# Reordering the start of a fused linear-attention and SwiGLU kernel: tile 1's K products, its scaled x, and tile 6's statistics

## The chip, the cores and the metric

The kernel runs on one core of a Trainium2 chip. The metric is the device time of one execution in microseconds (us), taken as the median of several runs. A profile of one further execution shows what each engine did: PE (the matrix engine; PEld is its weight load), ACT (ScalarE), DVE (VectorE), POOL (GpSimd) and SP (the queue that issues most of the DMAs).

## The reference

With x of 2048 rows by 512 columns in bf16, the output is x plus two branches of the same layer-normalised x:

```
def reference(A_x, A_wqkv, A_wo, B_x, B_w_gate, B_w_up, B_w_down):
    x = A_x                                   # (1, 2048, 512)
    xn = _layernorm(x, axis=-1)               # (x - mean) / sqrt(var + 1e-5)
    return x + _A_ref(xn, A_wqkv, A_wo) + _B_ref(xn, B_w_gate, B_w_up, B_w_down)

# A: linear attention, 32 heads of 16
    q, k, v = split(xn @ wqkv)
    phi = lambda t: where(t > 0, t + 1, exp(t)) + 1e-6
    pq, pk = phi(q), phi(k)
    kv = sum over s of pk (x) v;   z = sum over s of pk
    o = (pq @ kv) / (pq . z + 1e-6);   return o @ wo
# B: SwiGLU with F = 1792
    return (silu(xn @ w_gate) * (xn @ w_up)) @ w_down
```

## The kernel before, in words

The 2048 rows are 16 tiles of 128 rows. The program has three stretches. In the first, each tile gets its statistics, its normalised rows `xn`, their transposed form, the products for K and Q, and the feature map of K; and the sum over rows of xn (transposed) times pk is accumulated in four PSUM banks (`gtacc`, four matmuls a tile). In the second, the small matrices of the attention are made from that sum, while the SwiGLU products of the first 512 rows run. In the third, the SwiGLU products of the other 512-row blocks alternate with the output products of finished tiles.

All order is written out by hand. Every helper appends operations to one list per engine, and a small recorder (`_Prog`) adds the semaphore waits that the named tiles require. So the order of the calls in the program is, for each engine, the order in its queue, and an engine that waits holds everything behind it. Moving a call changes something only against the calls of the same engine. Two DMA issues hang on moved calls: `xn(t)` is `xn_dve(t)` followed, for tiles from 3 on, by a DMA transpose issued by SP.

The first tiles have a way of their own, and the change lies there. Tiles 0 to 3 don't wait for the inverse standard deviation before their products: `xc` is x minus the mean, it is transposed (tiles 0 to 2 by PE, with copies by ACT or DVE, called `tp_block`/`tc_block` and `tp_first`/`tc_first`; tile 3 by a DMA, `transpose_xc`), and K and Q are multiplied from it by `proj_part` (one product of 128 x 512, L499) or `proj_first` (two, L486). A K or Q of a tile is four such products over the four slices of the 512 columns, summed in one bank. The scale `rstd` then goes into ACT's evaluation of the bank: `first_ek` (exponential, L556), `first_pk` (Relu, L562), `first_pq` (L574). `clip_k` (L539, DVE) limits the exponential, and `first_feat` (L588, DVE; for tile 0 `feat_pool`, L581, on POOL) adds the two into pk. The normalised rows for `gtacc` are made by `xn_dve` (L316, DVE), which needs `rstd`. Tiles from 4 on are projected from the DMA-transposed `xn` (L472).

The statistics of a tile are `bns` (L299) and `agg` (L302) on DVE, then on POOL `eps` (L327) and `rstd_of` (L336), or `eps_two` (L344) and `rstd_two` (L353) for two tiles in one instruction each. The running sum of pk is `zsum` on POOL (L612 for tile 0, L616 for the rest). PE begins with eight matmuls on constants (`fill`, L271) until its first operands are there.

In the first stretch PE's order is: transposes of tiles 0 and 1, the 12 products of L499 (K of tiles 0 and 1, the first two Q products of each), transposes of tile 2, the four left of L499, K and Q of tile 2, `gtacc(0)`, K and Q of tile 3, `gtacc(1)`, `gtacc(2)`, and then K and Q of tile t followed by `gtacc(t-1)` for t = 4 and on.

Of the kernel before, what the change touches and what calls it, by code (L numbers as in the profile page):

```python
# [109 lines left out]
def bass_parallel_sum__linear_attn_block__swiglu_ffn__prompt_kernel(  # L110
# [13 lines left out]
    pe, act, dve, pool, sp = nc.tensor, nc.scalar, nc.vector, nc.gpsimd, nc.sync  # L124
    bf, f32 = dt.bfloat16, dt.float32

    with contextlib.ExitStack() as es:
# [64 lines left out]
        def bk(i):  # L192
            return ("bank", i)
# [10 lines left out]
        def xload(eng, h, t0, n, after=()):  # L204
            K.dma(
                eng, lambda: h.dma_start(x_sb[:, t0:t0 + n, :], rows(xin, t0, n)),
                r=list(after), w=[("x", t0 + i) for i in range(n)],
            )
# [89 lines left out]
        def bns(t):  # L298
            K.op("dve", lambda: dve.bn_stats(stats[:, t, :], x_sb[:, t, :]), r=[("x", t)], w=[("st", t)])  # L299

        def agg(t):
            K.op("dve", lambda: dve.bn_aggr(mv[:, t, :], stats[:, t, :]), r=[("st", t)], w=[("mv", t)])  # L302
# [10 lines left out]
        def xn_dve(t):  # L313
            K.op(
                "dve",
                lambda: dve.tensor_scalar(  # L316
                    out=xn_sb[:, t, :], in0=x_sb[:, t, :], scalar1=mv[:, t, 0:1], scalar2=rstd[:, t:t + 1],
                    op0=ALU.subtract, op1=ALU.mult,
                ),
                r=[("x", t), ("mv", t), ("rstd", t)], w=[("xn", t)],  # L320
            )

        def eps(t, eng):
            h = dve if eng == "dve" else pool
            K.op(
                eng,
                lambda: h.tensor_scalar(  # L327
                    out=vpe[:, t:t + 1], in0=mv[:, t, 1:2], scalar1=1e-5, scalar2=None, op0=ALU.add,
                ),
                r=[("mv", t)], w=[("vpe", t)],  # L330
            )

        def rstd_of(t):
            K.op(
                "pool",
                lambda: pool.tensor_tensor(out=rstd[:, t:t + 1], in0=vpe[:, t:t + 1], in1=nhalf[:, 0:1], op=ALU.pow),  # L336
                r=[("vpe", t), ("nhalf",)], w=[("rstd", t)],
            )

        def eps_two(t, eng):  # L340
            h = dve if eng == "dve" else pool
            K.op(
                eng,
                lambda: h.tensor_scalar(  # L344
                    out=vpe[:, t:t + 2], in0=mv[:, t:t + 2, 1], scalar1=1e-5, scalar2=None, op0=ALU.add,
                ),
                r=[("mv", t), ("mv", t + 1)], w=[("vpe", t), ("vpe", t + 1)],
            )

        def rstd_two(t):  # L350
            K.op(
                "pool",
                lambda: pool.tensor_tensor(  # L353
                    out=rstd[:, t:t + 2], in0=vpe[:, t:t + 2], in1=nhalf[:, :], op=ALU.pow,
                ),
                r=[("vpe", t), ("vpe", t + 1), ("nhalf",)], w=[("rstd", t), ("rstd", t + 1)],
            )
# [65 lines left out]
        def xc_full(t):  # L423
            K.op(
                "dve",
                lambda: dve.tensor_scalar(
                    out=xc_sb[:, t, :], in0=x_sb[:, t, :], scalar1=mv[:, t, 0:1], scalar2=None, op0=ALU.subtract,
                ),
                r=[("x", t), ("mv", t)], w=[("xc", t, 0), ("xc", t, 1)],
            )  # L430
# [8 lines left out]
        def tp_first(t, h, b):  # L439
            tb = banks[b].bitcast(bf)[:, 0:HD].rearrange("p (c s) -> p c s", c=2)  # L440
            K.op(
                "pe",
                [
                    (lambda c=c: pe.transpose(  # L444
                        tb[:, c, :], xc_sb[:, t, (2 * h + c) * P:(2 * h + c + 1) * P], ident[:, :],
                    ))
                    for c in range(2)
                ],
                r=[("xc", t, h), ("ident",)], w=[bk(b)],
            )  # L450

        def tc_first(t, h, b):
            tb = banks[b].bitcast(bf)[:, 0:HD].rearrange("p (c s) -> p c s", c=2)
            K.op(
                "act",
                lambda: act.activation(xcT[:, NDC * t + 2 * h:NDC * t + 2 * h + 2, :], tb, ACT.Copy),
                r=[bk(b)], w=[("xcT", t, 2 * h), ("xcT", t, 2 * h + 1)],
            )

        def transpose_dma(t):  # L460
            K.dma(
                "sp",
                lambda: sp.dma_start_transpose(out=xnT[:, :, t * P:(t + 1) * P], in_=xn_sb[:, t, :]),
                r=[("xn", t)], w=[("xnT", t)],
            )
# [15 lines left out]
        def proj_first(t, wname, h):  # L481
            lo, b = (D, kb(t)) if wname == "wk" else (0, qb(t))
            K.op(
                "pe",
                [
                    (lambda c=c: pe.matmul(  # L486
                        banks[b], xcT[:, NDC * t + c, :], wqkv_sb[:, c, lo:lo + D],
                        start=(c == 0), stop=(c == NDC - 1),
                    ))
                    for c in (2 * h, 2 * h + 1)  # L490
                ],
                r=[("xcT", t, i) for i in (2 * h, 2 * h + 1)] + [(wname, i) for i in (2 * h, 2 * h + 1)], w=[bk(b)],
            )

        def proj_part(t, wname, c, pos):
            lo, b = (D, kb(t)) if wname == "wk" else (0, qb(t))
            K.op(
                "pe",
                lambda: pe.matmul(  # L499
                    banks[b], xcT[:, NDC * t + c, :], wqkv_sb[:, c, lo:lo + D],  # L500
                    start=(pos == 0), stop=(pos == NDC - 1),
                ),
                r=[("xcT", t, c), (wname, c)], w=[bk(b)],
            )

        def kb(t):
            return 2 * (t % 2)

        def qb(t):
            return 2 * (t % 2) + 1  # L510
# [43 lines left out]
        def first_ek(t):  # L554
            K.op(
                "act", lambda: act.activation(ek[:, t % NE, :], banks[kb(t)], ACT.Exp, scale=rstd[:, t:t + 1]),  # L556
                r=[bk(kb(t)), ("rstd", t)], w=[("ek", t % NE)],
            )

        def first_pk(t):  # L560
            K.op(
                "act", lambda: act.activation(kpos[:, t % NE, :], banks[kb(t)], ACT.Relu, scale=rstd[:, t:t + 1]),  # L562
                r=[bk(kb(t)), ("rstd", t)], w=[("kpos", t % NE)],
            )
# [27 lines left out]
        def clip_k(t):  # L592
            clip(ek[:, t % NE, :], ("ek", t % NE))
# [14 lines left out]
        def zsum(t, after=()):  # L608
            pk = pkq[:, t, 0, :]
            after = list(after)  # L610
            if t == 0:
                K.op("pool", lambda: pool.tensor_copy(zacc[:, :], pk), r=[("pk", t)] + after, w=[("zacc",)])  # L612
            else:
                K.op(
                    "pool",
                    lambda: pool.tensor_tensor(out=zacc[:, :], in0=zacc[:, :], in1=pk, op=ALU.add),  # L616
                    r=[("pk", t), ("zacc",)] + after, w=[("zacc",)],
                )
# [20 lines left out]
        def xn(t):  # L639
            xn_dve(t)  # L640
            if t >= 3:
                transpose_dma(t)
# [12 lines left out]
        tc_block(0, 0, 4, "dve")  # L655
        tc_block(0, 1, 5, "act")
        tp_first(0, 1, 6)
        tc_first(0, 1, 6)
        eps(0, "pool")
        tp_first(1, 0, 7)  # L660
        tp_first(1, 1, 3)
        tc_first(1, 0, 7)
        bns(1)
        rstd_of(0)
        xn_dve(0)
# [7 lines left out]
        agg(3)  # L673
        proj_part(0, "wk", 0, 0)
        proj_part(0, "wk", 1, 1)
        proj_part(0, "wk", 3, 2)
        proj_part(0, "wk", 2, 3)
        first_ek(0)
        clip_k(0)
        xc_full(3)  # L680
        bns(4)
        proj_part(1, "wk", 0, 0)
        proj_part(1, "wk", 1, 1)
        proj_part(1, "wk", 3, 2)
        proj_part(1, "wk", 2, 3)
        proj_part(1, "wq", 0, 0)
        proj_part(1, "wq", 1, 1)
        transpose_xc(3)
# [9 lines left out]
        agg(4)  # L698
        bns(5)
        agg(5)  # L700
        bns(6)
        agg(6)
        proj_part(0, "wq", 2, 2)
        proj_part(1, "wq", 2, 2)
        proj_part(0, "wq", 3, 3)
# [1 line left out]
        proj_part(1, "wq", 3, 3)  # L707
        proj_first(2, "wk", 0)
        proj_first(2, "wk", 1)
        eps_two(1, "pool")  # L710
        rstd_two(1)
        first_ek(1)
        clip_k(1)
        first_pq(1)
# [3 lines left out]
        gtacc(0)  # L718
        eps_two(3, "pool")
        rstd_two(3)  # L720
        eps_two(5, "pool")
        rstd_two(5)
        xn(4)
        xload("sp", sp, 12, 2)
        xn_dve(1)
        first_pk(1)
        first_feat(1)
        proj_first(3, "wk", 0)
# [5 lines left out]
        first_pk(2)  # L734
        first_feat(2)
        xn(5)
        xn(6)
        first_pq(2)
        proj_first(3, "wk", 1)
        first_ek(3)  # L740
# [3 lines left out]
        gtacc(1)  # L744
        gtacc(2)
        xn_dve(3)
        zsum(0, [("xn", 3)])
        bns(7)
        kproj(4)
# [374 lines left out]
```

## Time and profile before

| what | value |
|---|---|
| median of 3 runs | 210.42 us (210.4 to 210.62) |
| profiled execution, its own time | 210.88 us |
| span of the profiled execution, first to last instruction | 209.6 us |
| PE busy | 206.9 us, 99% of the span |
| DVE busy | 120.3 us, 57% |
| ACT and POOL busy | 71.3 and 72.0 us, 34% each |
| chain that ended last | PE 97%, DMA 1%, DVE 1% |

A row of the timeline gives start, length, engine, source line, operation, output and inputs, and the count of instructions merged into the row; in brackets the idle time of the engine before it and what ended that. A matmul's length in the record covers its way through the array, so successive matmuls overlap in it; what they cost the engine is the distance between starts. In the waits, a row is engine, line, whom it waited for, total time, times, and the longest.

### The profile page before, as it was taken

The page shows a single profiled execution, that of the slowest core. Times are in us where ns is not written, and L with a number is a line of the kernel's source. Part 1 is how long each engine was busy: PE and PEld are TensorE (multiplying, and loading weights), DVE is VectorE, ACT ScalarE, POOL GpSimd, SP SyncE. Part 2 cuts the span into 40 slices and gives each one's busy share as a digit, 9 for nine tenths or more (in the row PEclk, how much of TensorE's full clock was granted, in tenths as well). Part 3 has the DMA queues.
Part 4 walks back from the last instruction along what each step waited for, and adds up shares of the span by engine and source line. Part 5 has one row for each costly group of instructions (what it writes and reads, how often), then busy time and mean ns, then how long its engine had stood idle before and what let it go on. Part 6 is the DMA issues. An engine that isn't in the chain of part 4 may idle for free.

```text
span 209.6 us, 2822 instructions
## 1 busy us (share of the span) xinstructions
PE 206.9 (99%) x1014; PEld 94.5 (45%) x1014; DVE 120.3 (57%) x246; ACT 71.3 (34%) x126; POOL 72.0 (34%) x90
## 2 busy tenths in 40 slices
PE   8999999999999999999999999999999999999996
PEld 3444444444444444444444444444444444444444
DVE  4989989335465874637355746365556535374122
ACT  6686666976543331302122312213031213121000
POOL 3526977658032443223141422240424132221200
DMA  6763644697797021010101110102011010110101
GB/s 201 225 179 71 127 78 100 175 377 240 192 359 68 2 46 26 29 25 25 50 2 50 28 25 25 50 0 53 2 48 25 27 28 25 46 32 25 50 28 50
DMA packets 30287, 16.84 MB, mean 80 GB/s; under 512 B 20928, under 2 KB 29632, under 8 KB 30272
## 3 DMA queue, kind: packets, MB, share of 16 engines
q1 hardware_dynamic: 29984, 16.39, 29.9%
q10 hardware_dynamic: 288, 0.26, 0.4%
q8 instruction: 8, 0.13, 0.3%
q14 instruction: 7, 0.06, 0.1%
HBM read 9.70 MB, written 2.10 MB: 56 GB/s over the span
## 4 chain that ended last, share of the span: by engine, by line
PE 97%; DMA 1%; DVE 1%; issue 0%
PE psum L821 46%; PE psum L1026 23%; PE psum L472 10%; PE psum L1015 7%; PE psum L624 7%; PE psum L499 2%; PE psum L486 2%; DMA x_sb<-in_A_x_dram 1%; PE psum L444 0%; DVE stats L299 0%; PE psum L928 0%; PE psum L410 0%; PE psum L951 0%; DVE xc_sb L380 0%; DVE out_sb L1039 0%
## 5 line engine op out<-in xcount | busy, mean ns | idle before, releaser
L836 ACT ACTIVATE sg<-psum 128x512 bf16<-128x512 f32 x56 | 33.4, 598 | 106.0 <-PE psum L821 103.6
L821 PE MATMUL psum<-xnT,wg_sb 128*128 128x512 bf16 x224 | 57.5, 379 | 0.0
L821 PE MATMUL psum<-xnT,wu_sb 128*128 128x512 bf16 x224 | 57.5, 379 | 0.0
L970 POOL TENSOR_TENSOR prod<-pkq,zb 128x512 f32<-128x512 bf16 x16 | 18.6, 1161 | 55.9 <-DVE pkq L548 55.9
L821 PEld LDWEIGHTS psum<-xnT,wu_sb 128*128 128x128 bf16 x224 | 21.9, 98 | 26.4
L821 PEld LDWEIGHTS psum<-xnT,wg_sb 128*128 128x128 bf16 x224 | 21.7, 98 | 26.2 <-issue 0.2
L1039 DVE TENSOR_TENSOR out_sb<-psum,x_sb 128x512 bf16<-128x512 f32 (+2 forms) x17 | 11.2, 660 | 35.9 <-PE psum L1026 35.9
L994 POOL TENSOR_TENSOR pqn<-pkq,rden 128x512 bf16<-128x512 bf16 x16 | 16.9, 1055 | 36.6 <-DVE rden L988 36.6
L842 DVE TENSOR_TENSOR pkq<-psum,sg 128x512 bf16<-128x512 f32 x28 | 19.2, 686 | 17.1 <-PE psum L821 14.7
L842 DVE TENSOR_TENSOR xn_sb<-psum,sg 128x512 bf16<-128x512 f32 x28 | 18.8, 671 | 14.2 <-PE psum L821 13.6
L1026 PE MATMUL psum<-wd_sb,xn_sb 128*128 128x512 bf16 (+2 forms) x126 | 25.7, 355 | 0.0
L1026 PE MATMUL psum<-wd_sb,pkq 128*128 128x512 bf16 x112 | 25.5, 379 | 0.0
L472 PE MATMUL psum<-wqkv_sb,xnT 128*128 128x512 bf16 x96 | 22.5, 379 | 0.0
L616 POOL TENSOR_TENSOR zacc<-zacc,pkq 128x512 f32<-128x512 f32 x15 | 17.3, 1155 | 5.0 <-DVE ek L539 4.6
L1026 PEld LDWEIGHTS psum<-wd_sb,xn_sb 128*128 128x128 bf16 x126 | 11.8, 98 | 12.5
L1026 PEld LDWEIGHTS psum<-wd_sb,pkq 128*128 128x128 bf16 x112 | 11.0, 98 | 13.2
L1015 PE MATMUL psum<-m_sb,eq 128*128 128x512 bf16 (+2 forms) x68 | 16.6, 366 | 0.0
L624 PE MATMUL psum<-pkq,xn_sb 128*128 128x512 bf16 x64 | 15.9, 379 | 0.0
L472 PEld LDWEIGHTS psum<-wqkv_sb,xnT 128*128 128x128 bf16 x96 | 9.4, 98 | 11.3
L978 DVE TENSOR_REDUCE den<-prod 128x32 f32<-128x512 f32 x16 | 10.9, 683 | 5.9 <-POOL prod L970 5.9
L299 DVE BATCH_NORM_STATS2 stats<-x_sb 128x6 f32<-128x512 bf16 x16 | 10.9, 679 | 3.3 <-DMA x_sb<-in_A_x_dram 3.3
L548 DVE SCALAR_TENSOR_TENSOR pkq<-pkq,eq 128x512 bf16<-128x512 bf16 x16 | 11.1, 693 | 0.6
(73 smaller groups left out, 139.3 us busy)
## 6 DMA issues: line engine op xcount, KB each, us to landing
out_dram<-out_sb SPq DMA_DIRECT2D x15, 128.0 KB, 1.7
wg_sb<-in_B_w_gate_dram SPq DMA_DIRECT2D x2, 896.0 KB, 8.2
wu_sb<-in_B_w_up_dram SPq DMA_DIRECT2D x2, 896.0 KB, 6.4
wd_sb<-in_B_w_down_dram SPq DMA_DIRECT2D x1, 1792.0 KB, 11.1
x_sb<-in_A_x_dram SPq DMA_DIRECT2D x5, 256.0 KB, 3.0
x_sb<-in_A_x_dram SPq DMA_DIRECT2D x5, 128.0 KB, 3.2
wqkv_sb<-in_A_wqkv_dram SPq DMA_DIRECT2D x5, 128.0 KB, 3.4
wqkv_sb<-in_A_wqkv_dram SPq DMA_DIRECT2D x1, 512.0 KB, 8.4
```

Of the source, the lines that this page charges most:

```text
L472: (lambda c=c: pe.matmul(banks[b], xnT[:, c, t * P:(t + 1) * P], wqkv_sb[:, c, lo:lo + D], start=(c == 0), stop=(c == NDC - 1),))
L548: lambda: dve.scalar_tensor_tensor(out=dst, in0=src, scalar=0.0, in1=e, op0=ALU.max, op1=ALU.add,),
L616: lambda: pool.tensor_tensor(out=zacc[:, :], in0=zacc[:, :], in1=pk, op=ALU.add),
L624: (lambda c=c: pe.matmul(banks[4 + c], xn_sb[:, t, c * P:(c + 1) * P], pkq[:, t, 0, :], start=(t == 0), stop=(t == NT - 1),))
L821: (lambda c=c: pe.matmul(banks[b], w_sb[:, c, fc * P:(fc + 1) * P], xnT[:, c, C * 512:(C + 1) * 512], start=(c == 0), stop=(c == NDC - 1),))
L836: lambda: act.activation(sg[:, j % NSG, :], banks[gb], ACT.Silu),
L842: lambda: dve.tensor_tensor(out=hT(C, fc), in0=banks[ub], in1=sg[:, j % NSG, :], op=ALU.mult,),
L970: lambda: pool.tensor_tensor(out=p, in0=pkq[:, t, 1, :], in1=zb[:, :], op=ALU.mult),
L994: lambda: pool.tensor_tensor(out=pqn[:, t % NPN, :].rearrange("p (i g h e) -> p g i h e", i=NB, g=NG, e=DH), in0=pkq[:, t, 1, :].rearrange ...
L1015: (lambda g=g: pe.matmul(dst, pqnT(t)[:, g, :], m_sb[:, g, lo:hi], start=(g == 0), stop=False,))
L1026: (lambda fc=fc: pe.matmul(dst, hT(C, fc)[:, jj * P:(jj + 1) * P], wd_sb[:, fc, lo:hi], start=False, stop=(fc == NFC - 1),))
L1039: lambda: dve.tensor_tensor(out=o, in0=src, in1=x_sb[:, t, lo:hi], op=ALU.add),
```

## The change

It moves calls and splits one pair of instructions; no operand, shape, buffer or transfer is changed.

- ACT: the copy of tile 0's second transposed half, `tc_first(0, 1, 6)`, goes behind the copy of tile 1's first half. PE's transposes keep their order.
- PE: tile 1's first two K products go ahead of tile 0's last two. Over the eight K products the order was 0,0,0,0,1,1,1,1 and becomes 0,0,1,1,0,0,1,1.
- DVE: tile 1's scaled x (`xn_dve(1)`) moves from behind tile 4's scaled x to behind tile 3's subtraction, ahead of tile 4's statistics. The calls for its `rstd` move up in the program.
- DVE: tile 6's statistics move from behind tile 5's to behind tile 5's scaled x, after tile 2's feature sum. Tile 6's scaled x, with its DMA transpose, moves from there to behind tile 3's scaled x.
- POOL: `rstd` of tiles 5 and 6, one pair of instructions for both, becomes a pair for each.

```
@@ (before the first products)
         tp_first(0, 1, 6)
-        tc_first(0, 1, 6)
         eps(0, "pool")
         tp_first(1, 0, 7)
         tp_first(1, 1, 3)
         tc_first(1, 0, 7)
+        tc_first(0, 1, 6)
@@ (K products)
         proj_part(0, "wk", 0, 0)
         proj_part(0, "wk", 1, 1)
+        proj_part(1, "wk", 0, 0)
+        proj_part(1, "wk", 1, 1)
         proj_part(0, "wk", 3, 2)
         proj_part(0, "wk", 2, 3)
+        proj_part(1, "wk", 3, 2)
+        proj_part(1, "wk", 2, 3)
         first_ek(0)
         clip_k(0)
         xc_full(3)
+        eps_two(1, "pool")
+        rstd_two(1)
+        xn_dve(1)
         bns(4)
-        proj_part(1, "wk", 0, 0)
-        proj_part(1, "wk", 1, 1)
-        proj_part(1, "wk", 3, 2)
-        proj_part(1, "wk", 2, 3)
@@ (statistics)
         bns(5)
         agg(5)
-        bns(6)
-        agg(6)
@@
-        eps_two(1, "pool")
-        rstd_two(1)
         first_ek(1)
@@
-        eps_two(5, "pool")
-        rstd_two(5)
+        eps(5, "pool")
+        rstd_of(5)
         xn(4)
         xload("sp", sp, 12, 2)
-        xn_dve(1)
         first_pk(1)
@@
         first_pk(2)
         first_feat(2)
         xn(5)
-        xn(6)
+        bns(6)
+        agg(6)
+        eps(6, "pool")
+        rstd_of(6)
@@
         gtacc(1)
         gtacc(2)
         xn_dve(3)
+        xn(6)
         zsum(0, [("xn", 3)])
```

More of the change, by code (lines that the diff above doesn't have):

```diff
@@ L657, in bass_parallel_sum__linear_attn_block__swiglu_ffn__prompt_kernel @@
         tp_first(0, 1, 6)
-        tc_first(0, 1, 6)
         eps(0, "pool")
@@ L662, in bass_parallel_sum__linear_attn_block__swiglu_ffn__prompt_kernel @@
         tc_first(1, 0, 7)
+        tc_first(0, 1, 6)
         bns(1)
@@ L675, in bass_parallel_sum__linear_attn_block__swiglu_ffn__prompt_kernel @@
         proj_part(0, "wk", 1, 1)
+        proj_part(1, "wk", 0, 0)
+        proj_part(1, "wk", 1, 1)
         proj_part(0, "wk", 3, 2)
         proj_part(0, "wk", 2, 3)
+        proj_part(1, "wk", 3, 2)
+        proj_part(1, "wk", 2, 3)
         first_ek(0)
@@ L680, in bass_parallel_sum__linear_attn_block__swiglu_ffn__prompt_kernel @@
         xc_full(3)
+        eps_two(1, "pool")
+        rstd_two(1)
+        xn_dve(1)
         bns(4)
[L682 to L685, printed above, removed]
         proj_part(1, "wq", 0, 0)
@@ L700, in bass_parallel_sum__linear_attn_block__swiglu_ffn__prompt_kernel @@
         agg(5)
-        bns(6)
-        agg(6)
         proj_part(0, "wq", 2, 2)
@@ L709, in bass_parallel_sum__linear_attn_block__swiglu_ffn__prompt_kernel @@
         proj_first(2, "wk", 1)
-        eps_two(1, "pool")
-        rstd_two(1)
         first_ek(1)
@@ L720, in bass_parallel_sum__linear_attn_block__swiglu_ffn__prompt_kernel @@
         rstd_two(3)
-        eps_two(5, "pool")
-        rstd_two(5)
+        eps(5, "pool")
+        rstd_of(5)
         xn(4)
         xload("sp", sp, 12, 2)
-        xn_dve(1)
         first_pk(1)
@@ L736, in bass_parallel_sum__linear_attn_block__swiglu_ffn__prompt_kernel @@
         xn(5)
-        xn(6)
+        bns(6)
+        agg(6)
+        eps(6, "pool")
+        rstd_of(6)
         first_pq(2)
@@ L746, in bass_parallel_sum__linear_attn_block__swiglu_ffn__prompt_kernel @@
         xn_dve(3)
+        xn(6)
         zsum(0, [("xn", 3)])
```

## The prediction

> **What bounds the kernel now.** I read the page first (busy time, chain), then the waits of the matmul engine, then PE's timeline for the first 21 us, and only then the engines whose queues the change edits. From the page:
>
> ```profile
> span 209.6 us, 2822 instructions
> PE 206.9 (99%) x1014; PEld 94.5 (45%) x1014; DVE 120.3 (57%) x246; ACT 71.3 (34%) x126; POOL 72.0 (34%) x90
> ...
> PE 97%; DMA 1%; DVE 1%; issue 0%
> ```
>
> PE is busy for 206.9 of 209.6 us and carries 97% of the chain. A busy PE could still hide holes, because a matmul's record is longer than its slot, so I look at starts. The only wait of PE in the whole span, and its timeline:
>
> ```profile
> PE psum L271 <- PEq L1109: 0.8, 1, 0.8
> 0.84 3.36 PE L271 MATMUL psum<-const-bfloat16-1.0 128*128 128x512 bf16 x8 [0.84 <-PEq L1109]
> 4.26 0.40 PE L410 MATMUL psum<-ident,xc_sb 128*128 128x128 bf16 x2
> 4.46 0.84 PE L444 MATMUL psum<-ident,xc_sb 128*128 128x128 bf16 x6
> 5.09 3.52 PE L499 MATMUL psum<-wqkv_sb,xcT 128*128 128x512 bf16 x12
> 8.45 0.39 PE L444 MATMUL psum<-ident,xc_sb 128*128 128x128 bf16 x4
> ...
> 12.12 1.89 PE L486 MATMUL psum<-wqkv_sb,xcT 128*128 128x512 bf16 x8
> ...
> 15.57 1.89 PE L472 MATMUL psum<-wqkv_sb,xnT 128*128 128x512 bf16 x8
> ...
> 19.89 1.03 PE L624 MATMUL psum<-pkq,xn_sb 128*128 128x512 bf16 x4
> ```
>
> Between 12.12 and 15.57 the timeline has sixteen products (eight of L486, eight of L624): 3.45 / 16 = 0.216 us each; from 15.57 to 19.89 twenty products (two projections of eight and one accumulation of four) take 4.32, again 0.216. The stream has no hole there. Only the beginning is slower: 12 products from 5.09 to 8.45 take 3.36. If the last eight go at 0.216 (1.73), the first four took 1.63, some 0.41 each. So PE doubles its rate at about 6.7 us and then works without a break to the end. An edit gains only if it shortens the time before 4.26 (it touches nothing there) or brings the rate up earlier; it loses if one of PE's operands becomes late.
>
> **Part 1: the product order.** The same 1014 matmuls are issued. Of the 12 products, positions 3 and 4 become tile 1's first two, 5 and 6 tile 0's last two. Starts, from the steps of 0.41 and 0.216: 5.09, 5.50, 5.91, 6.31, 6.72, 6.93, 7.15, 7.37. Who feeds them is ScalarE:
>
> ```profile
> 4.91 0.94 ACT L456 ACTIVATE xcT<-psum 128x256 bf16<-128x256 bf16 x3
> 6.92 0.69 ACT L556 ACTIVATE ek<-psum,rstd 128x512 bf16<-128x512 f32 x1 [1.08 <-PE psum L499]
> 7.50 0.68 ACT L562 ACTIVATE kpos<-psum,rstd 128x512 f32<-128x512 f32 x1
> 8.76 0.66 ACT L456 ACTIVATE xcT<-psum 128x256 bf16<-128x256 bf16 x2 [0.57 <-PE psum L444]
> ...
> 11.24 0.70 ACT L562 ACTIVATE kpos<-psum,rstd 128x512 f32<-128x512 f32 x1
> 11.99 0.23 PEld L486 LDWEIGHTS psum<-wqkv_sb,xcT 128*128 128x128 bf16 x2 [0.20 <-ACT kpos L562]
> 1.73 0.46 SPq L213 DMA_DIRECT2D wqkv_sb<-in_A_wqkv_dram  x1
> DMA to landing us min/median/max: 3.0/3.4/3.7
> ```
>
> The three copies are 0.28 apart and 0.38 long. Tile 1's first half now goes first, but its transposes are the third and fourth of the six at L444: six of them take 5.09 - 4.46 = 0.63, so the fourth starts at 5.09 - 3 x 0.105 = 4.77 and ends, like the sixth (4.98 to 4.46 + 0.84 = 5.30), 0.32 later, at 5.09. So that copy runs 5.12 to 5.50, tile 0's second half 5.40 to 5.78, tile 1's second half 5.68 to 6.06. Position 3 needs the first at 5.91, position 5 the second at 6.72, position 7 the third at 7.15. All have 0.4 us or more in hand: no hole. Weights: the slice issued at 1.73 lands by 1.73 + 3.7 = 5.43 even at the longest landing, and was needed at 6.31, now at 6.93. Nothing waited for it, so this slack buys nothing.
>
> What comes later is tile 0's finished K: its sixth product instead of the fourth, 6.93 + 0.38 = 7.31 instead of 6.88. The exponential (L556) moves from 6.92 to 7.35, the Relu (L562) from 7.50 to 7.94, ending 8.62. ScalarE's next work at 8.76 waits 0.57 us for PE, so it covers the 0.43, and ScalarE is unchanged from there on.
>
> **Part 2: VectorE.** Its queue is in order, so I walk it:
>
> ```profile
> 7.87 0.26 DVE L539 TENSOR_SCALAR ek<-ek 128x512 bf16<-128x512 bf16 x1
> 8.04 0.35 DVE L426 TENSOR_SCALAR xc_sb<-x_sb,mv 128x512 bf16<-128x512 bf16 x1
> 8.69 0.69 DVE L299 BATCH_NORM_STATS2 stats<-x_sb 128x6 f32<-128x512 bf16 x1 [0.30 <-DMA x_sb<-in_A_x_dram]
> ...
> 10.31 0.66 DVE L299 BATCH_NORM_STATS2 stats<-x_sb 128x6 f32<-128x512 bf16 x1
> ...
> 11.10 0.26 DVE L539 TENSOR_SCALAR ek<-ek 128x512 bf16<-128x512 bf16 x1
> 11.28 0.73 DVE L316 TENSOR_SCALAR xn_sb<-x_sb,mv,rstd 128x512 bf16<-128x512 bf16 x2
> 11.97 0.69 DVE L588 TENSOR_TENSOR pkq<-kpos,ek 128x512 bf16<-128x512 f32 x1
> ...
> 13.73 0.73 DVE L316 TENSOR_SCALAR xn_sb<-x_sb,mv,rstd 128x512 bf16<-128x512 bf16 x2
> 14.82 0.29 DVE L539 TENSOR_SCALAR ek<-ek 128x512 bf16<-128x512 bf16 x1 [0.35 <-ACT ek L556]
> 15.40 0.69 DVE L588 TENSOR_TENSOR pkq<-kpos,ek 128x512 bf16<-128x512 f32 x1 [0.29 <-ACT kpos L562]
> 16.01 0.41 DVE L316 TENSOR_SCALAR xn_sb<-x_sb,mv,rstd 128x512 bf16<-128x512 bf16 x1
> 16.33 0.69 DVE L299 BATCH_NORM_STATS2 stats<-x_sb 128x6 f32<-128x512 bf16 x1
> ...
> 18.66 0.68 DVE L548 SCALAR_TENSOR_TENSOR pkq<-psum,ek 128x512 bf16<-128x512 f32 x1
> 3.97 0.32 POOL L327 TENSOR_SCALAR vpe<-mv 128x1 f32<-128x1 f32 x1 [2.40 <-DVE mv L302]
> 4.37 0.65 POOL L336 TENSOR_TENSOR rstd<-vpe,nhalf 128x1 f32<-128x1 f32 x1
> 7.10 0.72 POOL L353 TENSOR_TENSOR rstd<-vpe,nhalf 128x2 f32<-128x2 f32 x1
> 8.28 1.16 POOL L581 TENSOR_TENSOR pkq<-kpos,ek 128x512 bf16<-128x512 f32 x1 [0.45 <-ACT kpos L562]
> 16.48 0.61 POOL L612 CAST zacc<-pkq 128x512 f32<-128x512 bf16 x1 [4.19 <-DVE xn_sb L316]
> ```
>
> The clip of tile 0 waits for the later exponential: 8.07 instead of 7.87, tile 3's subtraction 8.25, tile 1's scaled x 8.57 (one such takes 0.73 - 0.41 = 0.32 of the queue; its rstd is done at 7.82; moving that pair in the program changes nothing on POOL, where it already stood ahead of the sum at 8.28). The statistics of tile 4 start 8.89 instead of 8.69, since the 0.30 us wait for x takes most of the 0.32. SP's transpose of tile 3 goes out 0.2 later; that tile's first product, at 12.12, is over a microsecond behind its landing. Tile 6's statistics and aggregation (10.31 to 11.10: 0.79) and tile 1's scaled x (0.32) are gone here, so VectorE, 0.2 late at 10.5, does the clip of tile 1 and tile 4's scaled x and then idles some 0.6 us: the feature sum at 11.97 waits for ScalarE (11.24 + 0.70 = 11.94) and stays.
>
> After tile 5's scaled x at 13.73 come tile 6's statistics at 14.06, to 14.96; tile 3's clip at 14.88 instead of 14.82; its sum stays at 15.40, as that waits for ScalarE. The 0.35 and 0.29 us of idle time pay for the 0.79 together with tile 6's scaled x, which leaves. That lands behind tile 3's, at 16.33, so everything from the next statistics on is 0.32 later. POOL's two small steps for tile 6 (3.97 to 5.02 above: 1.05) run from 15.02 to 16.07, inside the 4.19 us hole before 16.48.
>
> Who waits for this 0.32? The tightest is tile 4's accumulation on PE at 19.89, which needs the operation of 18.66, ending 19.34. A weight load may start 0.13 before its product without a hole (11.99 and 12.12), 0.05 after its releaser (11.94 to 11.99): deadline 19.89 - 0.18 = 19.71. After the change it ends at 19.66: 0.05 to spare, of 0.37 before. Tile 6's DMA transpose goes out about 16.8 instead of 15.4, lands by about 19.4, and its projection starts at 19.89 + 0.86 = 20.75: 1.1 to spare once its weight load, 0.2 ahead of it, is counted.
>
> **The sum.** Before 4.26: 0. Positions 3 to 8: 0. ScalarE: +0.43, covered. VectorE: +0.32, covered with 0.05 left. PE's path: 0, bounded below at 0 by the stream without holes, and above by the rivals. The profiled execution took 210.88 us (span 209.6 and 1.28 around it); the median of the runs is 0.46 less, 210.42. Forecast: 210.4, no change; 0.2% (0.42 us) is about what a measurement of this kernel can tell from none.
>
> **Rivals.** Slower: tile 6's scaled x is caught by POOL's cast at 16.48, which starts as tile 3's scaled x ends. The trace has such a meeting:
>
> ```profile
> 34.00 1.15 POOL L616 TENSOR_TENSOR zacc<-zacc,pkq 128x512 f32<-128x512 f32 x1
> 34.07 1.23 DVE L316 TENSOR_SCALAR xn_sb<-x_sb,mv,rstd 128x512 bf16<-128x512 bf16 x1
> ```
>
> An operation of 0.41 took 1.23 and ended 0.15 after POOL's. The Trainium skill ("SBUF — State Buffer", section "SBUF: two separate sides") says the same: VectorE in a two-port mode and GpSimd share one pair of ports by an exclusive lock, and the later one blocks fully; this row agrees. Here it would end at 16.48 + 0.61 + 0.15 = 17.24 instead of 16.74; the shift becomes 0.82, and beyond 0.37 PE pays: 0.45, 210.9. It decides only if tile 6's rstd (due 16.07) comes after 16.33, or POOL starts first; by my times VectorE is 0.15 ahead. The same meeting at 8.57, behind the sum on POOL (now about 8.71, again second), would end 8.71 + 1.16 + 0.15 = 10.02 instead of 8.98; of that 1.04 the idle 0.6 before 11.97 and 0.2 before 15.40 take 0.8, and PE pays 0.24 - 0.05 = 0.19: 210.6, still no change. Chance of the first: 0.13.
>
> Faster: in the timed executions a weight slice comes late, which the profiled one does not show, and the new order covers it. It would have to land 0.85 past 5.10 (1.73 + 3.4) before PE waits at all, and 1.3 late to gain 0.42: 210.0. Against it stands the spread of three runs, 0.22. Chance 0.08.
>
> The change upsets the doubling of PE's rate: position 3 without its operand at 5.91 leaves a hole in the slow stretch. The fill began at 0.84 and the rate doubled at 6.7, 5.9 us; the same again at half rate would cost up to 2.9 (213.3). It needs the copy that is due at 5.50 to end after 5.9: chance 0.03. The Trainium skill ("TensorE: Matmul & The Clock Gate", Part 1) has a window of about 3.4 us that runs free of the kernel, so that the slow stretch would differ from run to run; by that the loss would be an estimated 1.7 us, and either kernel would scatter as much, which three runs within 0.22 us do not show.
>
> **Numbers.** No change 0.76, slower 0.16 (0.13 and 0.03), faster 0.08. Range 210.1 to 211.0: below, the lowest run (210.40) less 0.3; above, the caught operation (210.9) and 0.1 of scatter. The faster case and the upset rate stay outside, about 1 in 10.
>
> **What would show it.** Right: PE from 4.26 on in the same steps, the third product at its old start, the exponential of tile 0 near 7.35, tile 1's scaled x near 8.6, statistics of tile 7 near 16.65, and tile 4's accumulation still at 19.89. Wrong: a start of PE out of step at 5.9 or 19.89, an L316 of over 0.8 us near 16.3, or a doubling of the rate that moves.

## The result, and the profile after

The changed kernel takes 211.18 us in the median (210.81 to 211.89, 7 runs), the kernel before 210.33 us (209.93 to 210.62, 7 runs); the ratio is 1.0048, 95% interval 1.0033 to 1.0063. That is slower, and 0.18 us above the forecast's range. A second measurement, beside other experiments, gave 1.0025 (1.0013 to 1.0038), with a median of 210.93, which lies inside the range. The two estimates of the loss are half and a quarter of a per cent.

The page after, span, busy times and chain:

```profile
span 209.9 us, 2805 instructions
PE 205.5 (98%) x995; PEld 94.3 (45%) x1014; DVE 122.1 (58%) x246; ACT 71.4 (34%) x126; POOL 73.1 (35%) x92
...
PE 93%; DVE 3%; DMA 1%; issue 1%; POOL 1%; ACT 0%
```

(995 instead of 1014 matmuls: some records are missing, and an "issue" wait may stand where one is.) VectorE's share of the chain has risen from 1% to 3%. The waits of PE and its timeline say where:

```profile
PE psum L271 <- PEq L1111: 0.8, 1, 0.8
PE psum L624 <- DVE pkq L548: 0.6, 1, 0.6
...
5.11 3.04 PE L499 MATMUL psum<-wqkv_sb,xcT 128*128 128x512 bf16 x12
7.98 0.39 PE L444 MATMUL psum<-ident,xc_sb 128*128 128x128 bf16 x4
...
17.70 1.89 PE L472 MATMUL psum<-wqkv_sb,xnT 128*128 128x512 bf16 x8
20.20 1.04 PE L624 MATMUL psum<-pkq,xn_sb 128*128 128x512 bf16 x4 [0.61 <-DVE pkq L548]
```

There is one hole, at the very place that the prediction called the tightest: eight products from 17.70 would end their slots at 19.43, and tile 4's accumulation starts at 20.20, 0.77 later, released by VectorE's L548. The second thing to see is the beginning. The 12 products take 7.98 - 5.11 = 2.87 us, against 3.36 in the profile before: in this execution PE's rate doubled earlier, and PE came to this place 0.46 us sooner (19.43 against 19.89). Net 0.31, and the spans differ by 0.3.

VectorE and POOL in the same execution:

```profile
8.12 0.26 DVE L539 TENSOR_SCALAR ek<-ek 128x512 bf16<-128x512 bf16 x1
8.30 0.35 DVE L426 TENSOR_SCALAR xc_sb<-x_sb,mv 128x512 bf16<-128x512 bf16 x1
8.56 1.28 DVE L316 TENSOR_SCALAR xn_sb<-x_sb,mv,rstd 128x512 bf16<-128x512 bf16 x1
9.76 0.68 DVE L299 BATCH_NORM_STATS2 stats<-x_sb 128x6 f32<-128x512 bf16 x1
...
15.38 0.69 DVE L588 TENSOR_TENSOR pkq<-kpos,ek 128x512 bf16<-128x512 f32 x1
15.99 1.23 DVE L316 TENSOR_SCALAR xn_sb<-x_sb,mv,rstd 128x512 bf16<-128x512 bf16 x2
17.15 0.68 DVE L299 BATCH_NORM_STATS2 stats<-x_sb 128x6 f32<-128x512 bf16 x1
...
19.46 0.68 DVE L548 SCALAR_TENSOR_TENSOR pkq<-psum,ek 128x512 bf16<-128x512 f32 x1
```

```profile
8.54 1.16 POOL L581 TENSOR_TENSOR pkq<-kpos,ek 128x512 bf16<-128x512 f32 x1 [0.70 <-DVE ek L539]
...
15.50 1.01 POOL L336 TENSOR_TENSOR rstd<-vpe,nhalf 128x1 f32<-128x1 f32 x1
16.47 0.61 POOL L612 CAST zacc<-pkq 128x512 f32<-128x512 bf16 x1
```

Tile 1's scaled x starts 0.02 us after POOL's sum and takes 1.28 us; it ends at 9.84, 0.14 after the sum's 9.70. At 15.99 two scaled x (tiles 3 and 6) take 1.23 instead of 0.73: tile 6's `rstd` on POOL took 1.01 us and was ready only at 16.51, and the cast at 16.47 then held the operation. So the statistics of tile 7 start at 17.15 instead of the 16.65 that the prediction named, and L548 ends at 20.14 instead of 19.66.

### The profile page after: what moved, and what is told of

The parts are those of the page before. It is cut to its first block, busy times and chain, and to the rows that moved or that the text cites. A ratio compares the mean times of both kernels' runs of the same rounds, so it can differ in the third digit from the quotient of the medians.

```text
span 209.9 us, 2805 instructions
## 1 busy us (share of the span) xinstructions
PE 205.5 (98%) x995; PEld 94.3 (45%) x1014; DVE 122.1 (58%) x246; ACT 71.4 (34%) x126; POOL 73.1 (35%) x92
## 4 chain that ended last, share of the span: by engine, by line
PE 93%; DVE 3%; DMA 1%; issue 1%; POOL 1%; ACT 0%
PE psum L823 46%; PE psum L1028 23%; PE psum L472 8%; PE psum L1017 7%; PE psum L624 5%; PE psum L499 2%; DVE stats L299 1%; PE psum L486 1%; DMA x_sb<-in_A_x_dram 1%; DVE xn_sb L316 1%; POOL rstd L336 0%; PE psum L444 0%; DVE pkq L588 0%; DVE mv L302 0%; PE psum L930 0%
## 5 line engine op out<-in xcount | busy, mean ns | idle before, releaser
L823 PE MATMUL psum<-xnT,wu_sb 128*128 128x512 bf16 x216 | 55.8, 379 | 0.4
L624 PE MATMUL psum<-pkq,xn_sb 128*128 128x512 bf16 x63 | 15.7, 379 | 0.7 <-DVE pkq L548 0.6
L548 DVE SCALAR_TENSOR_TENSOR pkq<-pkq,eq 128x512 bf16<-128x512 bf16 x16 | 11.1, 692 | 0.6
```

The costliest lines, as they stand in the source:

```text
L624: (lambda c=c: pe.matmul(banks[4 + c], xn_sb[:, t, c * P:(c + 1) * P], pkq[:, t, 0, :], start=(t == 0), stop=(t == NT - 1),))
L823: (lambda c=c: pe.matmul(banks[b], w_sb[:, c, fc * P:(fc + 1) * P], xnT[:, c, C * 512:(C + 1) * 512], start=(c == 0), stop=(c == NDC - 1),))
```

## The experiments

A meeting is here an operation of VectorE and one of POOL at the same time, of which one takes longer than it does otherwise. The doubling is the moment at which PE's rate doubles; it is called early where the 12 products at L499 take 2.59 to 2.87 us (seven of the twelve profiles with fill) and late where they take 3.19 to 3.43 (the other five). Theory M: VectorE is late for tile 4's accumulation because of meetings with POOL, and this costs as far as PE is early. Rivals: O, the product order costs; S, the new places in VectorE's queue cost without any meeting.

**The parts alone, and a control.** The control is the kernel before, unchanged.

> The kernel before once more, as a control: ratio 1.000 within 0.15%. Its profile tells whether the doubling of PE's rate, 6.7 us in the first profile of this kernel and 5.8 in that of the changed one, belongs to the kernel or differs between executions: theory M says it differs between executions of the same program.

The control gave 1.0009 (0.9996 to 1.0022). Its profile begins so:

```profile
4.95 2.92 PE L499 MATMUL psum<-wqkv_sb,xcT 128*128 128x512 bf16 x12
7.71 0.39 PE L444 MATMUL psum<-ident,xc_sb 128*128 128x128 bf16 x4
...
10.52 1.03 PE L624 MATMUL psum<-pkq,xn_sb 128*128 128x512 bf16 x4
11.65 1.89 PE L486 MATMUL psum<-wqkv_sb,xcT 128*128 128x512 bf16 x8
```

2.76 us for the 12 products, where the first profile of the same program has 3.36. The moment of doubling differs from execution to execution; it does not belong to the kernel. The 35 runs of the kernel before that were taken beside these lie between 209.95 and 210.88 us. The kernel before isn't free of holes either: here the four products from 10.52 would end their slots at 11.38, and tile 3's K starts at 11.65. VectorE had waited 0.49 us for a tile of x in this execution; that tile 3's operand was late through it is likely, not shown.

Product order and copies alone (the first group of the diff and the proj_part lines of the second, without any line of VectorE or POOL; `...` marks lines left out, here and below):

```
         tp_first(0, 1, 6)
-        tc_first(0, 1, 6)
...
         tc_first(1, 0, 7)
+        tc_first(0, 1, 6)
...
         proj_part(0, "wk", 1, 1)
+        proj_part(1, "wk", 0, 0)
+        proj_part(1, "wk", 1, 1)
         proj_part(0, "wk", 3, 2)
...
```

> The kernel before with the product order and ScalarE's copies of the change alone; VectorE's and POOL's queues as before. Theory M (the loss is VectorE being late for tile 4's accumulation, after meetings with POOL): no hole on PE at 19.2 to 20.2, time within 0.2% of before (210.1 to 210.7). Rival O (the product order itself costs, by tile 0's later K): slower by 0.3% or more, 211.0, with the hole.

1.0004 (0.9993 to 1.0014), median 210.18 against 210.18. Rival O falls. Its profile shows what PE does when nothing holds it:

```profile
4.95 2.79 PE L499 MATMUL psum<-wqkv_sb,xcT 128*128 128x512 bf16 x12
7.58 0.39 PE L444 MATMUL psum<-ident,xc_sb 128*128 128x128 bf16 x4
...
19.03 1.03 PE L624 MATMUL psum<-pkq,xn_sb 128*128 128x512 bf16 x4
```

2.63 us, nearly 12 x 0.216: the doubling came before the first product, and tile 4's accumulation starts at 19.03, 0.86 earlier than in the first profile of the kernel before. The span is 208.8. Span less this start is 189.7 or 189.8 here, before, after and in the repeated profiles: so all that this change does to the time is done by then.

Tile 1's scaled x alone:

```
         xc_full(3)
+        eps_two(1, "pool")
+        rstd_two(1)
+        xn_dve(1)
         bns(4)
...
-        eps_two(1, "pool")
-        rstd_two(1)
...
-        xn_dve(1)
         first_pk(1)
```

> The kernel before with tile 1's scaled x alone moved behind tile 3's subtraction. Theory M: its L316 near 8.4 starts just after POOL's sum of tile 0 and takes about 1.2 us instead of 0.4; but VectorE's idle times before 11.97 and 15.40 take most of it up, and tile 6's scaled x still stands in its old place, so tile 4's accumulation keeps its start within 0.1 us: time within 0.2% of before. If the held operation alone makes the loss: slower by 0.3% or more. Rival O: no change, and L316 at 0.4 us.

1.0024 (1.0015 to 1.0032): slower, between the two values that the expectation named. The control's ratio, 1.0009, and its median, 210.51 us against 210.54 here, make the size of this loss doubtful; what is plainer is that the short runs are gone. Of the 35 runs of the kernel before 26 lie below 210.40 us, of the control's twelve six, of these twelve none, as M would have it if the loss falls on the executions in which PE is early. DVE, POOL and PE rows of its profile, and a wait of PE:

```profile
8.86 1.27 DVE L316 TENSOR_SCALAR xn_sb<-x_sb,mv,rstd 128x512 bf16<-128x512 bf16 x1
8.84 1.15 POOL L581 TENSOR_TENSOR pkq<-kpos,ek 128x512 bf16<-128x512 f32 x1 [0.45 <-DVE ek L539]
13.77 2.10 PE L624 MATMUL psum<-pkq,xn_sb 128*128 128x512 bf16 x8
PE psum L499 <- DMA wqkv_sb<-in_A_wqkv_dram: 0.5, 1, 0.5
```

The meeting is there, and the eight products at L624 (tiles 1 and 2) take 2.10 instead of 1.89: a hole of 0.2 that was not on my list, as tile 2's sum came late. But two landings were late in this execution as well: VectorE waited 0.45 us for a tile of x (its statistics at 6.26), and PE 0.49 us for a weight slice ahead of the 12 products. So this profile shows that the meeting happens; what it costs is read from the runs.

Tile 6's part alone:

```
-        bns(6)
-        agg(6)
...
-        eps_two(5, "pool")
-        rstd_two(5)
+        eps(5, "pool")
+        rstd_of(5)
...
         xn(5)
-        xn(6)
+        bns(6)
+        agg(6)
+        eps(6, "pool")
+        rstd_of(6)
...
         xn_dve(3)
+        xn(6)
```

> The kernel before with tile 6's statistics and scaled x alone moved (and its rstd pair split). Theory M: tile 6's rstd on POOL takes about 1.0 us instead of 0.6, its scaled x behind tile 3's starts late and takes 0.4 to 0.7, VectorE is 0.5 to 0.8 late at tile 7's statistics, and PE has a hole of 0.1 to 0.4 us before tile 4's accumulation: 210.4 to 210.8. Rival S (the added 0.32 us in the full stretch of VectorE is enough without any meeting): every L316 at 0.4, shift 0.32, hole under 0.1. Rival O: no change.

1.0019 (1.001 to 1.0029). The time fits M, but its one profile is of an execution with a late doubling (12 products in 3.20 us) and shows neither the long `rstd` nor a hole, both of which M had named without that condition; every L316 takes 0.41, as rival S has it. So for this part the mechanism isn't shown by its own trace.

**Taking the meetings away from the change.** Four kernels were measured side by side: the changed kernel once more; the same with POOL's sum of tile 0 also waiting for tile 1's scaled x (first pair of lines below); with that and the cast waiting for tile 6's scaled x (both pairs); and with only the cast waiting (second pair). No queue changes its order.

```
         def feat_pool(t):
-                r=[("kpos", t % NE), ("ek", t % NE)], w=[("pk", t)],
+                r=[("kpos", t % NE), ("ek", t % NE), ("xn", 1)], w=[("pk", t)],
...
-        zsum(0, [("xn", 3)])
+        zsum(0, [("xn", 6)])
```

> The changed kernel once more, beside the three that follow: ratio 1.004 to 1.006. Its profile tells whether the held L316 of tile 1 and the hole before tile 4's accumulation come again.

> The changed kernel, but POOL's sum of tile 0 (L581) waits for tile 1's scaled x, so that it cannot hold it; every queue keeps its order. Theory M: that L316 takes 0.41 instead of 1.28 us, VectorE is some 0.4 to 0.8 us earlier from tile 4's statistics on, the ratio falls from 1.005 to about 1.002, what tile 6's part alone cost. Rival S (the order of VectorE's queue costs, not the meeting): ratio stays at 1.004 or more.

> As the one before, and POOL's cast (L612) waits for tile 6's scaled x instead of tile 3's, so that it cannot hold that either. Theory M: no L316 over 0.5 us before 17 us, ratio 1.000 to 1.0015; what is left is the 0.32 us that tile 6's scaled x adds in the full stretch of VectorE, which costs only where PE's rate doubled early. Rival S: 1.004 or more.

> The changed kernel with only the second of these waits (the cast after tile 6's scaled x). Theory M: the L316 near 8.6 is still held (1.28), the one near 16.4 takes 0.41 instead of 0.68 where it met the cast; the ratio falls by at most 0.1%, to 1.0035 to 1.005. If the second meeting is the main cost: 1.002 or less.

Ratios against the kernel before: the changed kernel 1.0025 (1.0013 to 1.0038), below what I had expected; sum waiting 1.0012 (0.9999 to 1.0024); both waiting 1.0002 (0.999 to 1.0014); only the cast waiting 1.0017 (1.0005 to 1.0029). Only the cast waiting was expected at 1.0035 to 1.005 and came out lower, as did the changed kernel itself; its 1.0017 is under the 1.002 that was to mean that the second meeting is the main cost, but measured from 1.0025 it doesn't mean that. They fall in the order that M names, and with both meetings gone the order of the change costs nothing that can be measured. Set directly against each other, with twelve runs each, the changed kernel has a mean of 210.98 us and the one with both waits 210.62: 0.36 apart, with a 95% half width of 0.21. The queues are the same in both, so this speaks against S. The sum waiting alone takes off 0.30 (half width 0.20), the cast waiting alone 0.10 (0.22); the share of the second meeting isn't settled here. In the profile with only the cast waiting the first meeting (1.28) and PE's wait for L548 (0.57) come again. That with both waiting is of a late doubling (3.39), so no trace shows an early one without the meetings. The rows of the second kernel (sum waiting), DVE, POOL, and PE's wait:

```profile
8.21 0.41 DVE L316 TENSOR_SCALAR xn_sb<-x_sb,mv,rstd 128x512 bf16<-128x512 bf16 x1
...
14.57 0.69 DVE L588 TENSOR_TENSOR pkq<-kpos,ek 128x512 bf16<-128x512 f32 x1
15.18 1.23 DVE L316 TENSOR_SCALAR xn_sb<-x_sb,mv,rstd 128x512 bf16<-128x512 bf16 x2
14.69 1.01 POOL L336 TENSOR_TENSOR rstd<-vpe,nhalf 128x1 f32<-128x1 f32 x1
PE psum L624 <- DVE pkq L548: 0.2, 1, 0.2
```

The first meeting is gone (0.41), the second still there (1.23 for two), and PE still waits 0.2 us, not 0.6.

The repeated profile of the changed kernel itself turned out the most telling. PE, then DVE, then POOL:

```profile
5.06 3.35 PE L499 MATMUL psum<-wqkv_sb,xcT 128*128 128x512 bf16 x12
8.25 0.39 PE L444 MATMUL psum<-ident,xc_sb 128*128 128x128 bf16 x4
...
19.70 1.03 PE L624 MATMUL psum<-pkq,xn_sb 128*128 128x512 bf16 x4
```

```profile
8.35 0.41 DVE L316 TENSOR_SCALAR xn_sb<-x_sb,mv,rstd 128x512 bf16<-128x512 bf16 x1
...
15.20 0.70 DVE L588 TENSOR_TENSOR pkq<-kpos,ek 128x512 bf16<-128x512 f32 x1 [0.26 <-ACT kpos L562]
15.82 0.72 DVE L316 TENSOR_SCALAR xn_sb<-x_sb,mv,rstd 128x512 bf16<-128x512 bf16 x2
16.47 0.68 DVE L299 BATCH_NORM_STATS2 stats<-x_sb 128x6 f32<-128x512 bf16 x1
```

```profile
8.50 1.27 POOL L581 TENSOR_TENSOR pkq<-kpos,ek 128x512 bf16<-128x512 f32 x1 [0.70 <-DVE xc_sb L426]
...
15.17 0.58 POOL L336 TENSOR_TENSOR rstd<-vpe,nhalf 128x1 f32<-128x1 f32 x1
```

Here the doubling is late (3.19 us for the 12). VectorE is 0.15 ahead of POOL's sum, VectorE's operations take their normal time (POOL's sum 1.27 instead of 1.16), and PE has no hole. The time of this execution is 210.65 us; that it is less than the 210.88 of the first profile of the kernel before goes with PE's start at L499, 0.03 earlier, and its doubling, 0.17 earlier. That is the prediction's walk, with each mark some 0.2 us earlier; it happens in some executions only.

**Later PE.** Both kernels without the fill:

```
-        fill(7, 512)
-        fill(1, 256)
```

> The kernel before without the eight fill matmuls on constants (no result depends on them). PE's rate then doubles later in every execution, by the free time between 0.84 and 4.26. Theory M: 1 to 2 us slower than before (211.2 to 212.2), doubling after 7 us.

> The changed kernel without the eight fill matmuls. Theory M: what VectorE loses is lost only as far as PE is early; with PE a microsecond later the changed kernel ties with the kernel before in the same state, within 0.25% (0.5 us) of it, without a hole over 0.3 us at tile 4's accumulation. If the cost does not depend on when PE's rate doubles: slower than the kernel before without fill by 0.5% (1.0 us), as with fill.

The kernel before without fill takes 1.0083 (1.0066 to 1.0099), the changed one 1.0073 (1.0054 to 1.0092) of the kernel before; medians 212.26, just above the expected 212.2, and 212.03. With PE later, the changed kernel isn't measurably slower: the difference of the ratios is -0.0010, with the two half widths (0.0017 and 0.0019) combined +-0.0025. The single runs scatter over 1.6 us, and the means of the six runs are both 212.05, with a half width of some 0.7 us for their difference. That excludes the fixed cost of 1.0 us that the expectation named, but not safely one of a quarter per cent (0.5 us), which is what the second measurement of the changed kernel gave. The profile of the changed kernel without fill agrees with M: the 12 products take 4.39 us, tile 1's scaled x takes 0.41 at 9.09, ahead of POOL's sum at 9.25, and PE doesn't wait at tile 4's accumulation. That of the kernel before without fill is of its fastest run (211.04 us), with 3.51 us for the 12.

**Each part without its meeting,** on the kernel before:

> The kernel before with tile 1's scaled x alone moved, and POOL's sum of tile 0 made to wait for it. Theory M: without the meeting this move costs nothing: ratio 0.9995 to 1.001, against 1.0024 with it. Rival S (the place in VectorE's queue costs): 1.002 or more.

> The kernel before with tile 6's part alone, and POOL's cast made to wait for tile 6's scaled x instead of tile 3's. Theory M: the second meeting is gone, but tile 6's rstd can still be late where PE's rate doubled early: ratio 1.000 to 1.0015, against 1.0019 with the meeting. Rival S: 1.0019 or more.

Tile 1's move with the sum waiting: 0.9992 (0.998 to 1.0003), against 1.0024 (1.0015 to 1.0032) without that wait. The intervals are apart, and the short runs are back: eight of these twelve lie below 210.40 us (of the kernel before beside them, 12 of 23), against none of twelve. The meeting, not the place in the queue, makes the loss of this part. DVE, POOL and PE rows, to be read beside those of this move above:

```profile
8.37 0.41 DVE L316 TENSOR_SCALAR xn_sb<-x_sb,mv,rstd 128x512 bf16<-128x512 bf16 x1
8.93 1.15 POOL L581 TENSOR_TENSOR pkq<-kpos,ek 128x512 bf16<-128x512 f32 x1 [1.09 <-DVE xn_sb L316]
13.04 1.89 PE L624 MATMUL psum<-pkq,xn_sb 128*128 128x512 bf16 x8
```

Tile 6's part with the cast waiting: 1.0003 (0.9992 to 1.0015) against 1.0019 (1.001 to 1.0029). It falls as expected, but the intervals overlap, and its profile is again of a late doubling: that the meeting makes the loss of this part is likely, not shown. No version is faster than the kernel before beyond its interval; the nearest is tile 1's move with the sum waiting, median 210.03 against 210.34.

## Why the prediction was wrong

**The sum was made on one execution, and that one was at the edge.** "PE doubles its rate at about 6.7 us" was read as a constant of the kernel. Over the profiles with fill the 12 products took from 2.59 to 3.43 us, so PE arrives at tile 4's accumulation up to 0.86 us earlier than in the one I had. The step that failed first is therefore the term "0.05 to spare, of 0.37 before": the 19.71 deadline is 19.25 in the profiled execution of the changed kernel. I had the warning in hand: the Trainium skill ("TensorE: Matmul & The Clock Gate", Part 1) says that the window runs free of the kernel and that the slow stretch differs from run to run. I set it aside because three runs agreed within 0.22 us. Two later sets of 35 runs of the kernel before spread over 0.93 and 1.15 us (209.85 to 211.0 in the wider), and the repeated profiles of both programs agree with the Trainium skill here (3.36 and 2.76 us, 2.87 and 3.19).

**The order of the first meeting was the wrong way round.** The prediction named this meeting and its price, and put VectorE 0.14 us ahead. That margin rested on tile 0's late Relu. (The walk also gave tile 3's subtraction 0.32 us of the queue; the rows give it 0.26, so the margin would have been 0.20.) When PE doubles early, the Relu is done early, and POOL's sum is released by VectorE's own clip: it starts 0.15 us after the clip's end (8.54 after 8.12 + 0.26 = 8.38; the same with tile 1's move alone and with only the cast waiting), while the scaled x, one subtraction later in the queue, starts 0.18 after it (8.56). POOL is ahead by 0.02 to 0.03 us in all three profiles with the meeting. With the old product order the Relu is early even at a late doubling: in the first profile of the kernel before it ends at 8.18 and the clip at 8.13, so a scaled x there would have come at an estimated 8.30, just behind POOL's sum at 8.28. That may be why tile 1's move alone costs as much as the whole change; no run tests it. The 1.28 us were near the forecast (an end 0.15 after POOL's operation); "210.6, still no change" did not hold, because it spent the idle time of VectorE that an early PE takes away.

**The second meeting was the named slower rival, with 0.13.** Place, price and point of decision were right: it decides "only if tile 6's rstd (due 16.07) comes after 16.33", and it came at 16.51. What was mis-sized is the term "1.05" for POOL's two steps: 15.19 to 16.51 is 1.32, as the second of them took 1.01 beside VectorE's L588 and L316, which I had not counted among the meetings. Undisturbed the two steps take 0.89 (14.86 to 15.75 in the repeated profile). This too hangs on the doubling. Where it is late, tile 3's sum (L588) waits for ScalarE, and in all five profiles of this kind with tile 6's part the `rstd` starts 0.03 or 0.04 us ahead of the sum and takes 0.58. Where it is early, the sum doesn't wait, starts 0.12 us ahead of the `rstd`, and the `rstd` takes 1.01, in all three. The shift of VectorE came to 20.14 - 19.66 = 0.48 beyond the forecast; with PE 0.46 early and 0.05 to spare that makes 0.89 at the deadline. The hole is 0.77, since the product started 0.06 after its release (20.14 to 20.20) and not the 0.18 that the deadline allowed.

**Right:** the product order cost nothing, the landings of the weights gave the new order nothing to gain over twelve runs (though a late slice does occur: PE's 0.49 us in the profile of tile 1's move), ScalarE's 0.43 us were covered, and the tightest place of the change was tile 4's accumulation. In the late-doubling execution of the changed kernel each of the marks stands: L556 at a late start (7.16), no L316 over 0.41, no hole. The two rivals should not have stood as separate small chances: both, and the vanished slack, hang on the same early doubling, which seven of the twelve profiles with fill show.

## What to carry to other kernels

Slack read from one profile is slack in one execution: before a term is closed with 0.05 us to spare, ask which clock or landing differs from run to run, and redo the walk for the other end of its range. When two engines share a release, compare who starts first by the hand-off each needs (0.15 us across engines here, 0.18 through one more instruction in the queue): a wait that lets the short operation go first took the loss of tile 1's move away here.

## What the runs showed of the hardware

The moment at which PE's rate doubles differed between executions of one program: the same 12 products took 3.36 and 2.76 us in two profiles of the kernel before, 2.87 and 3.19 in two of the changed one. A small POOL operation is no small partner in a meeting: the `rstd` of 128x1 took 1.01 us where VectorE's sum of two inputs had begun 0.12 us before it, and 0.58 where it began 0.03 us before that sum (15.17 and 15.20 in the repeated profile). The order of the starts alone doesn't settle it: an `rstd` of two tiles (L353) that began at 11.73, 0.02 us before such a sum, took 1.48 us with tile 1's move and the sum waiting. The Trainium skill ("SBUF — State Buffer", section "SBUF: two separate sides") names both kinds of VectorE operation, two-port modes and two inputs, as holders of the shared ports; the rows at 8.56 and 15.50 agree. The rows at 15.17 and 15.20 do not show the full blocking that it states, since the sum took its normal 0.70 us beside the `rstd`.
